# A gated recurrence and a projection block: activation steps of one turn spread over the turns before it

## The chip, the cores and the metric

The kernel runs on one core of a Trainium2 chip. Its time is the device time of one execution in microseconds (us). The kernel before took 618.1 us, the median of three runs (617.54 to 618.85); the profiled run took 618.29 us, with a span of 616.6 us from its first instruction to its last.

## The reference

Two blocks follow one another, all in float32.

```
q, k, v, f_logit: (4, 8, 768, 48)        f = sigmoid(f_logit)
state = 0                                 per batch and head, 48 x 48
for t in 0 .. 767:
    state = f[t][:, None] * state + k[t][:, None] * v[t][None, :]
    y[t]  = q[t] @ state
x   = y, heads side by side: (3072, 384)
h   = x @ w_in                            (384 x 2048)
g   = h * erf(softplus(h))
out = g @ w_out                           (2048 x 384)
```

The weights w_in and w_out arrive as float64, and the kernel receives their words as pairs of 32-bit integers; it turns them into float32 itself, and the text calls that rounding.

## The kernel before, in words

**Tiling.** The 3072 rows are cut into 24 chunks of 128 tokens (index g) and 12 blocks of two chunks (index blk). A chunk goes through four stages. `stage_d` (L381) multiplies the logarithms of the gates with a triangle to sum them, takes two exponentials on ScalarE (`dp`, `kd`, L390 and L393) and scales q and k on VectorE (L402, L406); from chunk 3 on it also copies rows of `dp` to `Tall` by small transfers (L398). `stage_t` (L410) transposes both on TensorE (L418) and copies the result out of PSUM on ScalarE (`qA`, L425; `kT`, L427 or, from chunk 9, VectorE at L429); ahead of that it finishes the state of the chunk before (`next_state`, L445 and L446). `stage_s` (L450) computes scores and state contributions (L467, L475). Chunks 3 to 9 have the scores copied on ScalarE (L495) and masked on GpSimd (L498), later ones on VectorE (L503). `stage_y` (L511) computes y (L532), which ScalarE copies into `xT` (L536). The tiles of `stage_t` and `stage_y` come from a PSUM pool of two buffers, `ps_at`, so that y(g) uses the buffer that L425 of stage_t(g+1) has emptied.

**The second block.** `hidden(blk, gi)` (L585) computes a group of four 128-wide slices of h for 256 rows, 12 matmul steps (L594), and ScalarE copies it to SBUF (L601). A group is named (blk, gi), with gi from 0 to 3. Its PSUM pool `ps_moe` has two buffers. The function h * erf(softplus(h)) is computed from one exponential, three tanh and three products by `activate` (L546): exp (L157), two tanh terms (L160), two products on VectorE (`times`, L165), three empty steps, a last tanh (L566) and the product that ends in h (L568). The tile `e` has two buffers, so the exp of a group waits for the last product of the group two before it. `project_first` (L673, blocks 0 and 1) multiplies h with w_out plainly (L684); `project` (L701, later blocks) uses a scheme of seven products instead of eight (L735), for which `sum_w` and `sum_h` form sums on VectorE (L622). The sums of w_out go to the tile `wT`, over the h of block 0, which lies there too.

**What sets the order.** The order on each engine is written out by hand in one long loop (from L937). Its turn `it` runs from 0 to 11. In a turn a generator gives out matmul steps, called slots (counter `s`). Turn 0 computes hidden(0) and hidden(1) in 96 slots, turn 1 hidden(2) in 48, turn 2 hidden(3) in 48 and then project_first(0) in 32, turn 3 project_first(1) in 32 and then hidden(4) in 48; later turns hold project(it - 2) and hidden(it + 1). After each slot the loop may emit other work:
- a weight-rounding step (`weights_step`, L851), when the counter `due` reaches 1. A piece of a weight matrix (there are 8 of each) takes an absolute value on ScalarE (L311) and six operations on VectorE (L313 to L336). The w_in pieces have to be done ahead of the hidden groups that use them, the w_out pieces ahead of project_first.
- a load of a w_out piece (`load_more`, L868, L292), if the place where its raw words go is free.
- one stage of the recurrence, from the list `todo` at the slots in `at`.
- the logarithms of a later block's gates (`clamp`, L357, on VectorE and `logs`, L363, on ScalarE). Logarithm and tanh need different tables in ScalarE, which are loaded where they change (`ACT_TABLE_LOAD`, at L347 and L160).
- a step of the activations (`act_step`, L574). A step moves every running group on by one operation. A new group starts when the last one has made five steps, so in the long run five steps carry one group.
- from turn 2 on, a step of the sums (`sum_step`, L655).

Where a consumer is reached and its group isn't finished, the steps that it lacks are emitted at that place:

```
while not gr["done"]:
    act_step()
```

This stands in `project_first` (L682) and in `sum_h` (L642).

Of the kernel before, what the change touches and what calls it, by code (L numbers as in the profile page):

```python
# [74 lines left out]
def kernel(  # L75
# [741 lines left out]
    with tc.manual_schedule():  # L817

        for t in svs:
            nc.vector.memset(t[:].rearrange("p r c a d -> p (r c a d)"), 0.0)  # L820
        use_exp_ln()
        load_f(0)
        load(0, "kv", nc.scalar)
        load(0, "q")
        load_f(1)
        load(1, "qk")
        load_f(2)
        load_piece(0)
        load(1, "v")
        load(2)  # L830
        load_piece(1)
        load_piece(2)
        load_f(3)
        nc.gpsimd.memset(tri[:], 1.0)
        nc.gpsimd.affine_select(
            out=tri[:], in_=tri[:], pattern=[[1, P]], compare_op=ALU.is_ge, fill=0.0,
            base=0, channel_multiplier=-1,
        )
        nc.gpsimd.memset(tri[0:C, C:P], 0.0)
        for c in range(2):  # L840
            nc.gpsimd.tensor_copy(out=tri1[half(c), :], in_=tri[half(c), half(c)])
        make_identity(nc, ident)
        for t in dps:
            nc.vector.memset(t[:, :, D:DP], 1.0)
        for t in [qd] + kds:
            nc.vector.memset(t[:, :, D:DP], 0.0)

        to_round = deque(ORDER)
        in_work = []

        def weights_step():  # L851

            if not in_work or len(in_work) == 1 and in_work[0][2] == 5:
                if to_round:
                    i = to_round.popleft()
                    in_work.append([round_piece(i), i, 1])
                    next(in_work[-1][0], None)
            if in_work:
                r = in_work[0]
                r[2] += 1  # L860
                if next(r[0], "end") == "end":
                    rounded.add(r[1])
                    in_work.pop(0)


        to_load = [n_pieces + j for j in (3, 4, 0, 5, 1, 6, 2, 7)]

        def load_more():  # L868
            if to_load and home_free(to_load[0]):
                load_piece(to_load.pop(0))  # L870

        def load_to(g):
            while loaded[0] <= min(g, n_chunks - 1):
                load(loaded[0])
                loaded[0] += 1


        LOOK = 3
        loaded = [2 * LOOK]
        def weights_steps(n):  # L880
            for _ in range(n):
                weights_step()

        busy.append(ps_moe.tile([P, 2, 512], FP32, name="busy", tag="moe")[:, 0, 0:P])
        keep_busy(10)
        prepare(0, 0, 1)
        stage_d(0)
        keep_busy(6)
        prepare(0, 1, 2)
        stage_t(0)  # L890
        load(3, "qk")
        load_piece(3)
        stage_d(1)
        prepare(1, 0, 1)
        load_f(4)
        load_f(5)
        load_sv(0)
        stage_s(0)
        weights_steps(2)
        stage_t(1)  # L900
        load(4, "qk")
        load_piece(4)
        stage_d(2)
        load_sv(1)
        weights_steps(2)
        stage_y(0)
        load_sv(2)
        load(3, "v")
        load(5, "qk")
        load_piece(5)  # L910
        stage_s(1)
        weights_steps(2)
        stage_t(2)
        stage_y(1)
        prepare(1, 1, CPB)
        load_sv(3)
        load(4, "v")
        load_piece(6)
        weights_steps(4)


        def stages(blk):
            todo = [(stage_s, blk * CPB)] if blk == ADJACENT else []
            for g in range(blk * CPB, (blk + 1) * CPB):
                last = g == n_chunks - 1
                if blk >= ADJACENT:
                    todo += [(stage_y, g)] if last else [(stage_d, g + 1), (stage_t, g + 1), (stage_y_s, g)]
                    continue
                todo += [] if last else [(stage_d, g + 1)]
                todo += [(stage_s, g)]  # L930
                todo += [] if last else [(stage_t, g + 1)]
                todo += [(stage_y, g)]
            return todo

        check = check_decays()
        due = 0.0
        for it in range(n_blocks):  # L937
            gen, n = slots(it)
            if it == 0:
                todo = [(stage_s, 2), (stage_y, 2), (stage_d, 3), (stage_t, 3), (stage_s, 3), (stage_y, 3),  # L940
                        (stage_d, 4), (stage_t, 4), (stage_d, 5), (stage_s, 4), (stage_t, 5),
                        (stage_y, 4)] + stages(2)[4:]
                at = [1, 5, 6, 12, 16, 23, 34, 42, 48, 52, 60, 74, 76, 80, 88, 94]
            else:
                todo = stages(it + 2) if it + 2 < n_blocks else []
                at = [n * x // 48 for x in (2, 6, 11, 17, 25, 29, 34, 41)] if it == 1 else [int(3 + (n - 13) / max(1, len(todo)) * i) for i in range(len(todo))]
            if ADJACENT <= it + 2 < n_blocks:

                at = [0, 1, 15, 24, 31, 52, 66] if it + 2 == ADJACENT else [2, 26, 42, 54, 76, 90]
                at = at[: len(todo)]  # L950
            if it + 3 < n_blocks:
                prepare_at = at[todo.index((stage_d, (it + 3) * CPB))] - 14
            at, todo = deque(at), deque(todo)
            for s, _ in enumerate(gen):
                due += (1 if s < 42 else 0.6 if s < 72 else 0.3) if it == 0 else 0.42 if it == 1 else 0.6
                while due >= 1:
                    weights_step()
                    due -= 1
                if s % 6 == 3:
                    load_more()  # L960
                if at and s == at[0]:
                    at.popleft()
                    f, g = todo.popleft()
                    f(g)
                    if f in (stage_y, stage_y_s):
                        if g + NSV < n_chunks:
                            load_sv(g + NSV)
                        load_to(g + LOOK)
                        if g == 2:
                            load(5, "v")  # L970
                            load_piece(7)
                if it == 0 and s == 14:
                    prepare(2, 0, CPB)
                if it == 0 and s == 9:
                    load_f(6)
                    load_f(7)
                if s == n // 2 and it + 4 < n_blocks:
                    for j in range(CPB):
                        load_f((it + 4) * CPB + j)
                if it + 3 < n_blocks and s == prepare_at - 6:  # L980
                    clamp(it + 3, 0, CPB)
                if it + 3 < n_blocks and s == prepare_at:
                    logs(it + 3, 0, CPB)
                if it < 2:
                    step = it == 1 and s % 6 == 3
                elif it == 2:
                    step = s % 5 in (1, 3)
                elif it == 3:
                    step = s % 7 in (1, 4)
                elif it == n_blocks - 1:  # L990
                    step = s % 3 == 1
                else:
                    step = s % 9 in (2, 6)
                if step:
                    act_step()
                if it == 2:
                    if s % 2:
                        sum_step()
                elif it > 2:
                    if s == n - n_h and it < n_blocks - 1:  # L1000
                        to_sum.extend(sum_h(groups[it - 1, gi]) for gi in range(NS))
                    if it == n_blocks - 1 and s % n_o == 40 and s < 2 * n_o:
                        blk = n_blocks - 2 + s // n_o
                        to_sum.extend(sum_h(groups[blk, gi]) for gi in range(NS))
                    if it == 3:
                        if s % 2:
                            sum_step()
                    elif s < n_o or s % 3 == 0 or it == n_blocks - 1:
                        sum_step()
                if it == n_blocks - 2 and s in (5, 40):  # L1010
                    next(check)
            assert not todo
        assert len(rounded) == 2 * n_pieces
# [213 lines left out]
```

## Time and profile before

| engine | busy us | share of the span |
|---|---|---|
| TensorE, matmul | 588.3 | 95% |
| TensorE, weight load | 514.5 | 83% |
| VectorE | 459.7 | 75% |
| ScalarE | 382.9 | 62% |
| GpSimd | 14.9 | 2% |

TensorE carries 74% of the chain that ended last, VectorE 11% and ScalarE 8%. The largest group of instructions is the hidden matmul (L594), with 264.7 us. The longest wait between compute engines is ScalarE's exp (L157) for VectorE's product (L568), 57.6 us in 31 waits. A hidden slot is two records of L594 in the profile, since each float32 matmul shows twice; the same holds for L684 and L735. An instruction's time is given from its start; the idle time ahead of it stands in brackets in a timeline, with the engine and line that ended it. "issue" means that the profile shows no releaser.

### The profile page before, as it was taken

How to read it: one execution, taken by the hardware profiler on the slowest of the kernel's cores; microseconds unless marked ns; L12 is line 12 of the kernel's file. 1: busy time of each engine (PE TensorE's matmuls, PEld its weight loads, DVE VectorE, ACT ScalarE, POOL GpSimd, SP SyncE). 2: the span in 40 equal slices, each digit the busy share in tenths (PEclk: the TensorE clock that was granted, in tenths of full speed). 3: DMA queues.
4: the chain of work that ended last, by engine and by line, in shares of the span. 5: the costliest groups of instructions: out<-in, count | busy, mean ns of one | idle time of the engine just before them, and what ended most of it. 6: DMA issues, size and time to landing. Idle time of an engine off the chain costs nothing.

```text
span 616.6 us, 13769 instructions
## 1 busy us (share of the span) xinstructions
PE 588.3 (95%) x5729; PEld 514.5 (83%) x5729; DVE 459.7 (75%) x785; ACT 382.9 (62%) x483; POOL 14.9 (2%) x33
## 2 busy tenths in 40 slices
PE   8778799999999999999999999999999999999996
PEld 7556688887655689989989988988988989989996
DVE  4898998697489597896896875896886795656651
ACT  5735365987875678875866585875775666366000
POOL 1000011010000000000000000000000000000000
PEclk9987899999999999999999999999999999999999
DMA  9998753441241222133133132042130000000000
GB/s 201 248 228 208 199 175 63 71 88 17 53 77 28 41 63 52 25 81 54 33 71 53 32 73 53 14 91 53 15 65 15 3 27 0 28 1 0 27 27 30
DMA packets 155604, 41.36 MB, mean 67 GB/s; under 512 B 147344, under 2 KB 150416, under 8 KB 155536
## 3 DMA queue, kind: packets, MB, share of 16 engines
q1 hardware_dynamic: 153312, 39.82, 29.6%
q8 instruction: 47, 0.77, 0.5%
q10 hardware_dynamic: 2224, 0.59, 0.4%
q14 instruction: 21, 0.17, 0.1%
HBM read 35.59 MB, written 4.72 MB: 65 GB/s over the span
## 4 chain that ended last, share of the span: by engine, by line
PE 74%; DVE 11%; ACT 8%; DMA 3%; issue 2%; SPq 1%; POOL 0%; DVEq 0%; ACTq 0%; POOLq 0%
PE hps L594 31%; PE ops L735 25%; PE ops L684 7%; PE y L532 3%; PE ps_t L418 3%; PE ps_d L387 2%; ACT x L160 2%; PE sc L467 1%; PE sc L475 1%; DVE sv L445 1%; DVE sv L446 1%; DVE w_in_sb L322 1%; DVE Hg L568 1%; DVE w_in_sb L336 1%; PE busy L379 1%
## 5 line engine op out<-in xcount | busy, mean ns | idle before, releaser
L594 PE MATMUL hps<-xT,w_in_sb 128*128 128x256 f32 x1152 | 264.7, 386 | 5.0 <-DVE w_in_sb L336 2.9
L594 PEld LDWEIGHTS hps<-xT,w_in_sb 128*128 128x128 f32 x1152 | 218.5, 193 | 39.2 <-ACT xT L536 2.8
L165 DVE SCALAR_TENSOR_TENSOR e<-x,e 128x1024 f32<-128x1024 f32 x96 | 117.1, 1220 | 13.2 <-ACT x L160 12.6
L160 ACT ACTIVATE x<-Hg,serf_bias 128x1024 f32<-128x1024 f32 x88 | 97.5, 1140 | 0.2
L157 ACT ACTIVATE e<-Hg 128x1024 f32<-128x1024 f32 x44 | 46.5, 1058 | 61.7 <-DVE Hg L568 57.6
L735 PE MATMUL ops<-wT,Hg 128*128 128x192 f32 x320 | 78.4, 328 | 0.0
L568 DVE TENSOR_TENSOR Hg<-Hg,e 128x1024 f32<-128x1024 f32 x44 | 53.7, 1222 | 22.6 <-ACT e L566 22.5
L735 PE MATMUL ops<-wT,scratch 128*128 128x192 f32 x288 | 67.8, 326 | 0.9 <-DVE scratch L743 0.9
L735 PE MATMUL ops<-w_out_sb,Hg 128*128 128x192 f32 x320 | 65.1, 326 | 0.0
L601 ACT COPY Hg<-hps 128x1024 f32<-128x1024 f32 x44 | 44.4, 1010 | 32.7 <-PE hps L594 32.4
L735 PEld LDWEIGHTS ops<-wT,Hg 128*128 128x128 f32 x320 | 55.7, 190 | 1.9
L735 PEld LDWEIGHTS ops<-w_out_sb,Hg 128*128 128x128 f32 x320 | 54.6, 190 | 2.0
L566 ACT ACTIVATE e<-e 128x1024 f32<-128x1024 f32 x48 | 50.3, 1048 | 1.9 <-DVE e L165 1.8
L735 PEld LDWEIGHTS ops<-wT,scratch 128*128 128x128 f32 x288 | 50.2, 190 | 1.1 <-issue 1.1
L503 DVE TENSOR_TENSOR qA<-sc,tri 64x256 f32<-64x256 f32 x68 | 28.7, 422 | 27.3 <-PE sc L475 26.3
L743 DVE TENSOR_TENSOR scratch<-scratch,ops 128x384 f32<-128x384 f32 (+1 forms) x41 | 20.3, 494 | 29.5 <-ACT scratch L751 23.0
L532 PEld LDWEIGHTS y<-qA,sv 128*32 128x32 f32 x1536 | 24.9, 113 | 19.6 <-issue 12.4
L532 PE MATMUL y<-qA,sv 128*32 128x64 f32 x1536 | 29.9, 226 | 10.9 <-issue 5.1
L425 ACT COPY qA<-ps_t 64x512 f32<-64x512 f32 x48 | 27.7, 577 | 19.4 <-PE ps_t L418 19.0
L402 DVE TENSOR_TENSOR qd<-qn,dp 128x384 f32<-128x384 f32 x24 | 13.4, 556 | 33.6 <-ACT dp L390 33.5
L735 PE MATMUL ops<-w_out_sb,scratch 128*128 128x192 f32 x144 | 34.7, 326 | 0.0
L445 DVE TENSOR_TENSOR sv<-sc,sv 48x192 f32<-48x192 f32 x80 | 28.3, 354 | 8.3 <-ACT qA L495 6.9
(111 smaller groups left out, 648.1 us busy)
## 6 DMA issues: line engine op xcount, KB each, us to landing
lt<-in_f_logit_dram SPq DMA_DIRECT2D x24, 192.0 KB, 3.7
qn<-in_q_dram SPq DMA_DIRECT2D x24, 192.0 KB, 3.4
kn<-in_k_dram SPq DMA_DIRECT2D x23, 192.0 KB, 3.7
vt<-in_v_dram SPq DMA_DIRECT2D x23, 192.0 KB, 3.7
out_dram<-scratch SPq DMA_DIRECT2D x11, 384.0 KB, 2.6
sv<-in_v_dram SPq DMA_DIRECT2D x84, 48.0 KB, 2.8
w_out_sb<-in_moe_w_in_dram SPq DMA_DIRECT2D x4, 768.0 KB, 6.1
Hg<-in_moe_w_in_dram SPq DMA_DIRECT2D x4, 768.0 KB, 6.6
```

The lines of the kernel that those rows point to most:

```text
L157: nc.scalar.activation(out=dst[:], in_=h, func=AF.Exp)
L160: nc.scalar.activation(out=dst[:], in_=h, func=AF.Tanh, bias=serf_bias[:, i : i + 1], scale=SERF_KAB[i][0])
L165: nc.vector.scalar_tensor_tensor(out=e[:], in0=x[:], scalar=SERF_KAB[i][2], in1=e[:], op0=ALU.add, op1=ALU.mult)
L445: nc.vector.tensor_tensor(out=new, in0=add, in1=old, op=ALU.add)
L503: nc.vector.tensor_tensor(out=qA[half(1 - r), r, :, half(c)], in0=sc[half(c), r], in1=tri1[half(c)].unsqueeze(1).broadcast_to((C, HP, C)), ...
L532: nc.tensor.matmul(y[M * i : M * (i + 1), kt, half(c)], lhsT=sv[:, r, c, a, o : o + M], rhs=qA[:, r, a, half(c)], start=(n == 0), stop=Tru ...
L566: nc.scalar.activation(out=e[:], in_=e[:], func=AF.Tanh, scale=SERF_C)
L568: nc.vector.tensor_tensor(out=h, in0=h, in1=e[:], op=ALU.mult)
L594: nc.tensor.matmul(hps[:, j, :], lhsT=w_in_sb[:, kt, ft * P : (ft + 1) * P], rhs=xTs[blk][:, kt, :], start=(kt == 0), stop=(kt == n_k - 1),)
L601: nc.scalar.copy(out=gr["h"], in_=hps[:])
L684: nc.tensor.matmul(ops[:, tt, 0:d_model], lhsT=gr["h"][:, j, tt * P : (tt + 1) * P], rhs=w_out_sb[:, ft, :], start=(ft == 0), stop=(ft == ...
L735: nc.tensor.matmul(place[n], lhsT=x[:, j, :], rhs=y, start=(gi == 0 and j == 0 and n in first), stop=(gi == n_g - 1 and j == 1), skip_grou ...
```

## The change

Three settings of the loop change. In turns 0 and 1 activation steps are emitted where there were none or fewer: in turn 0 from slot 72 on at every eighth slot, in turn 1 at every fifth instead of every sixth. Turn 2 takes the rule of turn 3: two of seven slots instead of two of five. The aim is to even ScalarE's work out over the turns. Loads of w_out are tried in every odd slot instead of every sixth. Rounding goes at half a step per slot in turns 1 and 2, instead of 0.42 and 0.6.

```diff
-                due += (1 if s < 42 else 0.6 if s < 72 else 0.3) if it == 0 else 0.42 if it == 1 else 0.6
+                due += (1 if s < 42 else 0.6 if s < 72 else 0.3) if it == 0 else 0.5
                 while due >= 1:
                     weights_step()
                     due -= 1
-                if s % 6 == 3:
+                if s % 2:
                     load_more()
...
-                if it < 2:
-                    step = it == 1 and s % 6 == 3
-                elif it == 2:
-                    step = s % 5 in (1, 3)
-                elif it == 3:
+                if it == 0:
+                    step = s >= 72 and s % 8 == 5
+                elif it == 1:
+                    step = s % 5 == 3
+                elif it < 4:
                     step = s % 7 in (1, 4)
```

## Prediction

> **What bounds the kernel now.** I read the slices first. TensorE's first six slices (to about 92 us) hold sevens and eights while VectorE stands at 8 to 9; from then on TensorE is at 9 nearly everywhere.
>
> ```profile
> PE   8778799999999999999999999999999999999996
> ...
> DVE  4898998697489597896896875896886795656651
> ACT  5735365987875678875866585875775666366000
> ```
>
> So time can be won or lost only where TensorE waits. Next came busy times over turns 0 to 3, cut where the first matmul of a turn starts (columns: window; its length; busy us of PE, PEld, DVE, ACT, POOL; clock; DMA share; GB/s).
>
> ```profile
> 39.30:105.50 66.20, 58.94 (x590) 48.19 (x588) 62.00 (x99) 35.03 (x57) 5.56 (x8) 0.91 0.67 169
> 105.50:134.90 29.40, 28.98 (x374) 24.19 (x373) 20.95 (x37) 27.01 (x39) 3.15 (x4) 1.00 0.42 73
> 134.90:189.40 54.50, 50.59 (x438) 36.38 (x437) 39.68 (x58) 42.43 (x52) 2.99 (x4) 1.00 0.28 50
> 189.40:239.60 50.20, 50.20 (x486) 37.35 (x485) 39.10 (x64) 36.37 (x42) 0.50 (x2) 1.00 0.27 56
> ```
>
> Turn 0 belongs to VectorE: 62.00 of 66.20 us, nearly all weight rounding, which the change doesn't reduce. Turn 1 costs TensorE 0.42 us, turn 3 nothing. Turn 2 is where it stands idle, with ScalarE as the cause. In the timeline, y(8) (L532) starts when the copy L425 of stage_t(9) ends, because its PSUM buffer is the one that L425 empties; L425 stands behind an exponential, which waited 2.44 us for a product:
>
> ```profile
> 149.45 1.06 ACT L157 ACTIVATE e<-wT 128x1024 f32<-128x1024 f32 x1 [2.44 <-DVE wT L568]
> ...
> 150.51 1.17 ACT L425 COPY qA<-ps_t 64x512 f32<-64x512 f32 x2
> ...
> 151.78 1.37 PE L532 MATMUL y<-qA,sv 128*32 128x64 f32 x64 [1.37 <-issue]
> ```
>
> y(9) at 176.36 waits 1.51 us in the same way. A slot is two matmul records: 0.4317 us in hidden (96 records in 20.72 us), 0.648 us in project_first (28 in 9.03). One d, s, t and y take 0.65, 1.0, 0.87, 1.03. Turn 2 without a wait: 48 x 0.4317 + 32 x 0.648 + 2 x 3.55 = 48.6 us. It takes 54.5, so 5.9 us are lost: 3.8 before project_first starts at 164.67, 2.1 after.
>
> **What the skill says.** "TensorE: Matmul & The Clock Gate", Architectural detail: VectorE and ScalarE queues are strictly first in, first out; the 2.44 us above, passed on to L425, agrees. "ScalarE: Activation LUTs", What ACT_TABLE_LOAD costs: about 1.28 us to load, 1.38 more to drain; here a load takes 1.28 and the next instruction follows 0.02 later, so I use 1.28. The same page, Table sets: exponential and logarithm share one set, exponential and tanh another; so a logs call (L347) between two tanh costs two loads, as the trace shows (203.47, 207.43).
>
> **The change part by part.**
>
> *w_out's loads.* Slots 9 to 51 become 7 to 33. No abs (L311) or rounding step of w_out in the trace waited for a transfer, so nothing is won. Against that, about 4.6 MB are queued from 59.6 us ahead of stage_d(4)'s Tall rows; at 240 GB/s (the window's rate) they are gone at about 79, and the rows land near 81 instead of 77. Needed at 83.54 (L445): hidden, cost 0, at worst 3.
>
> *Rounding.* 0.42 to 0.5 steps per slot ends it at slot 37 of turn 1, not 44. Seven steps of 0.5 to 1.0 us come earlier on VectorE; their cost is in T2 below.
>
> *Steps moved.* I counted them slot by slot with the loop's conditions. Turn 0 gets 3 (0 before), turn 1 gets 9 (8), turn 2 gets 23 (32). Turn 0: exp at slot 77 and two tanh terms at 85 and 93, 1.06 + 1.28 + 1.16 + 1.16 = 4.7 us on ScalarE from 95 to 105, into gaps of 1.87, 1.55 and 2.28 us; L425 of stage_t(6) slips 0.9 but y(5) at 104.00 still finds it done. Cost 0. ScalarE's table loads stay equal in number.
>
> Turn 1, laid out by hand from these durations: L425 of stage_t(7) ends near 115.9, so y(6) no longer waits (-0.42). At the end, exp(1,0) at slot 38 waits for the product of (0,0), which VectorE finishes near 134.1; xT of y(7) is behind it and lands at 135.6 instead of 133.06. Turn 2's first matmul reads it. T2 = 135.7 against 134.92: +0.8 net. Bounds: -0.4 to +1.5.
>
> Turn 2, first part: 14 steps instead of 19 in 48 slots leave ScalarE 11 operations of 1.05 us instead of 15. L425 of stage_t(9) ends near 148.3 with y(8) due at 150.7; the copy of h(3,1) is done at 154.6, needed at 154.8. So 3.5 of the 3.8 us come back; y(9) is free too.
>
> *A wait that the change adds.* project_first's loop runs act_step until its group is done. Before, (0,3) was done at slot 66, needed at 72. With 23 steps it still lacks two. At slot 72 they are emitted immediately ahead of the matmul: tanh, then on VectorE sum_w(2)'s first step (slot 71, overwriting a part of wT that slot 69's matmul reads), times (L165) of (1,2), then the product (L568). From slot 69's end, 1.3 us before slot 72: 0.15 + 0.55 + 1.14 + 1.22 = 3.06, so TensorE stands 1.85 us with the release. If sum_w must wait for slot 71 it is 3.15. Nothing of before shows this wait; I take 1.85, since slot-wise addresses decide it. TensorE's queue behind it holds the rest of project_first. Turn 2's second part: 2.1 lost before, 1.85 now.
>
> T3 = 135.7 + 25.9 + 0.3 + 22.5 + 1.85 = 186.25 against 189.44: 3.2 us ahead.
>
> *A second one, larger.* Before, (1,3)'s tanh is at slot 11 of turn 3, ahead of logs(6) at slot 17. Now it is at slot 22, behind it, and its product is forced at slot 24, where project_first(1) needs it. ScalarE before, after stage_t(11):
>
> ```profile
> 202.28 1.17 ACT L425 COPY qA<-ps_t 64x512 f32<-64x512 f32 x2 [4.69 <-PE ps_t L418]
> 203.47 1.28 ACT L347 ACT_TABLE_LOAD   x1
> 204.76 0.84 ACT L367 ACTIVATE lt<-lt 128x768 f32<-128x768 f32 x1
> 205.64 0.84 ACT L368 ACTIVATE lt<-lt 128x768 f32<-128x768 f32 x1
> ...
> 207.43 1.28 ACT L160 ACT_TABLE_LOAD   x1
> 208.73 1.15 ACT L160 ACTIVATE x<-Hg,serf_bias 128x1024 f32<-128x1024 f32 x1
> ```
>
> Afterwards: L425 1.19, term 1.12, load 1.29, logs 1.65, load 1.29, term 1.06, tanh 1.04 = 8.64 from L425's start, then the product and two hand-overs, 1.4: 10.0. L425 starts 0.7 after stage_t, so slot 24 can start 10.7 us after it; TensorE gets there after 0.87 + 8 x 0.648 = 6.06. Wait: 4.65 us (bounds 3.8 to 5.5). It is tied to stage_t(11), so ScalarE can't work ahead of it.
>
> *A third, passed on.* term and tanh of groups (2,1) and (2,0) now follow the output copy L694 and d(12) (slots 32 and 33), which wait for TensorE, instead of running before. exp(2,2) comes 1.35 us later against TensorE, and the ping-pong exp, tanh, product keeps that lag until L425 of stage_t(12). Before, that copy was just in time:
>
> ```profile
> 230.38 1.15 ACT L425 COPY qA<-ps_t 64x512 f32<-64x512 f32 x2
> ...
> 231.71 0.81 PE L532 MATMUL y<-qA,sv 128*32 128x64 f32 x42
> ```
>
> With 0.1 slack: +1.25 (bounds 0 to 2). From slot 36 of turn 3 the orders are equal, and nothing more differs.
>
> Sum: -3.2 + 4.65 + 1.25 = +2.7. 618.1 + 2.7 = 620.8 us.
>
> **Rivals.**
> - *Forced steps find everything ready* (ends faster): each costs one product and hand-over, 1.3. Recovered 5.9 - 0.3 - 0.8 = 4.8, minus 2.6, minus 1.25: 617.1. For it: ScalarE idles 4.69 us before 202.28. Against: the chain starts only after stage_t(11).
> - *A wash*: xT of y(7) in time (-0.8) and no third wait (-1.25): 618.7, down to 618.1 with a shorter second wait.
> - *More is lost*: sum_w waits for slot 71 (+1.3) and turn 2's copies of h lag on (+1): 623.1.
> - *Loads collide*: Tall rows late, VectorE's queue and turn 0 shift by 3: 623.8. Against: 2 us of slack, and most of the shift would be absorbed where VectorE waits 3.01 us at 108.5.
>
> **How the numbers follow.** Forecast 0.64, more is lost 0.12, loads collide 0.04, wash 0.11, all ready 0.09. The likeliest gives 620.8. Its own terms reach from 619.3 to 622.5; with the wash below and the larger loss above the range is 618.5 to 623.4. Faster by over 0.2% (under 616.9): 0.06. Within 0.2% (to 619.3): 0.13. Slower: 0.81.
>
> **What would show it.** Right: idle TensorE of 4 to 5 us in front of project_first(1)'s last group, released by L568; one of 2 to 3 in front of project_first(0)'s last group; no wait ahead of y(8) and y(9); ScalarE's tanh of (1,3) behind the two table loads; L532 of y(11) waiting for L425. Wrong: the product of (1,3) ends before stage_t(11); or y(8) still waits; or turn 0 ends at another time than 105.5.

## The result and the profile after

The changed kernel takes 621.8 us (median of 4 runs, 621.25 to 622.39) against 618.12 us before. The ratio is 1.0059, with a 95% interval of 1.0042 to 1.0077: 3.7 us slower, where the prediction had 2.7 us in a range of 618.5 to 623.4.

The slices of the span show little, because the changes are small against a slice of 15.5 us. TensorE's row now has a 7 in the fourteenth slice, and the row of the granted clock, which the prediction did not look at, has an 8 at the same place.

```profile
PE   8778799999999799999999999999999999999996
...
PEclk9987899999999899999999999999999999999999
```

A clock of 0.50 in the text below means that TensorE was granted half of its full speed.

The windows of the prediction, on the new trace (window; its length; busy us of PE, PEld, DVE, ACT, POOL; clock; DMA share; GB/s):

```profile
39.30:105.50 66.20, 58.99 (x590) 48.34 (x588) 62.02 (x99) 39.39 (x61) 5.58 (x8) 0.90 0.64 167
105.50:134.90 29.40, 29.17 (x374) 23.91 (x372) 23.03 (x36) 24.03 (x37) 3.08 (x4) 1.00 0.42 73
134.90:189.40 54.50, 53.22 (x508) 38.45 (x508) 38.35 (x62) 39.36 (x52) 3.80 (x4) 1.00 0.30 57
189.40:239.60 50.20, 44.44 (x396) 32.39 (x395) 34.66 (x55) 33.34 (x38) 0.50 (x2) 0.97 0.18 35
```

ScalarE took on 4.4 us in turn 0 (35.03 to 39.39) at no cost to TensorE: d(7) starts at 107.12 us, before at 107.13. In the third window TensorE has 508 instructions instead of 438. Most of its idle time has moved into the fourth window: 5.8 us there, where it had none, and 1.3 us left in the third.

TensorE's timeline has all the waits that matter in a few lines. The number in brackets is the idle time ahead of a piece, with what ended it.

```profile
135.41 2.00 PE L594 MATMUL hps<-xT,w_in_sb 128*128 128x256 f32 x8 [0.29 <-ACT xT L536]
...
150.82 1.10 PE L532 MATMUL y<-qA,sv 128*32 128x64 f32 x64
...
161.99 4.03 PE L684 MATMUL ops<-w_out_sb,wT 128*128 128x384 f32 x12
...
171.99 1.10 PE L532 MATMUL y<-qA,sv 128*32 128x64 f32 x64
173.02 6.72 PE L684 MATMUL ops<-w_out_sb,wT 128*128 128x384 f32 x20
180.72 5.43 PE L684 MATMUL ops<-w_out_sb,wT 128*128 128x384 f32 x16 [0.99 <-DVE wT L568]
185.99 0.81 PE L684 MATMUL ops<-w_out_sb,Hg 128*128 128x384 f32 x2
...
199.01 5.33 PE L684 MATMUL ops<-w_out_sb,Hg 128*128 128x384 f32 x16
208.92 1.65 PE L684 MATMUL ops<-w_out_sb,Hg 128*128 128x384 f32 x2 [4.58 <-DVE Hg L568]
210.50 1.94 PE L532 MATMUL y<-qA,sv 128*32 128x64 f32 x64
...
235.92 1.10 PE L532 MATMUL y<-qA,sv 128*32 128x64 f32 x64 [1.17 <-ACT qA L425]
```

y(8) and y(9), at 150.82 and 171.99, no longer wait; project_first starts at 161.99 instead of 164.67 and turn 3 at 185.99 instead of 189.44. That is the gain. The losses follow: 1.2 us at 180.72 (due at 173.02 + 10 x 0.648 = 179.50), 4.7 us at 208.92 (due at 199.01 + 8 x 0.648 = 204.19), and 1.2 us at 235.92. There is a fourth: the two matmul records at 208.92 need 1.65 us where two records of the same shape need 0.91 elsewhere (the x2 piece at 187.71), and y(10) needs 1.94 us against 1.10 for y(9). The window from 208.92 us has the reason in its clock column:

```profile
204.20:208.90 4.70, 0.14 (x1) 0.00 (x0) 1.26 (x2) 3.38 (x4) 0.00 (x0) 1.00 0.00 0
208.92:212.36 3.44, 3.44 (x66) 2.19 (x66) 1.08 (x1) 0.00 (x0) 0.50 (x2) 0.50 0.00 0
212.40:220.00 7.60, 7.60 (x75) 5.26 (x72) 3.72 (x10) 4.32 (x7) 0.00 (x0) 1.00 0.56 110
```

After 4.7 us without work TensorE ran 3.44 us at a clock of 0.50, so 1.72 us were lost behind the wait.

ScalarE's part of the second wait, on the changed kernel, answers to the lines at 202.28 us of before:

```profile
198.83 1.17 ACT L425 COPY qA<-ps_t 64x512 f32<-64x512 f32 x2 [1.84 <-PE ps_t L418]
200.03 1.15 ACT L160 ACTIVATE x<-Hg,serf_bias 128x1024 f32<-128x1024 f32 x1
201.19 1.28 ACT L347 ACT_TABLE_LOAD   x1
...
204.22 1.28 ACT L160 ACT_TABLE_LOAD   x1
205.51 1.15 ACT L160 ACTIVATE x<-Hg,serf_bias 128x1024 f32<-128x1024 f32 x1
206.57 1.04 ACT L566 ACTIVATE e<-e 128x1024 f32<-128x1024 f32 x1
```

The tanh of (1,3), the last line, stands behind two table loads; the product follows at 207.64 on VectorE and TensorE at 208.92.

### The profile page after: what moved, and what is told of

Its sections match the earlier page's. It is cut to its first block, busy times and chain, and to the rows that moved or that the text cites. A ratio compares the mean times of both kernels' runs of the same rounds, so it can differ in the third digit from the quotient of the medians.

```text
span 620.6 us, 13769 instructions
## 1 busy us (share of the span) xinstructions
PE 589.7 (95%) x5729; PEld 515.4 (83%) x5729; DVE 459.9 (74%) x785; ACT 382.4 (62%) x483; POOL 15.7 (3%) x33
## 4 chain that ended last, share of the span: by engine, by line
PE 75%; DVE 10%; ACT 8%; DMA 2%; SPq 2%; issue 1%; POOL 0%; DVEq 0%; ACTq 0%; POOLq 0%
PE hps L594 33%; PE ops L735 25%; PE ops L684 5%; PE y L532 3%; PE ps_t L418 3%; ACT x L160 2%; PE ps_d L387 2%; PE sc L467 1%; PE sc L475 1%; DVE Hg L568 1%; ACT e L566 1%; ACT e L157 1%; DMA kn<-in_k_dram 1%; SPq L398 1%; DVE w_in_sb L336 1%
## 5 line engine op out<-in xcount | busy, mean ns | idle before, releaser
L532 PEld LDWEIGHTS y<-qA,sv 128*32 128x32 f32 x1536 | 25.2, 116 | 17.8 <-issue 9.1
L532 PE MATMUL y<-qA,sv 128*32 128x64 f32 x1536 | 30.2, 230 | 8.8 <-ACT qA L425 2.4
L425 ACT COPY qA<-ps_t 64x512 f32<-64x512 f32 x48 | 27.7, 576 | 16.0 <-PE ps_t L418 15.6
```

What stands on the lines that cost most here:

```text
L532: nc.tensor.matmul(y[M * i : M * (i + 1), kt, half(c)], lhsT=sv[:, r, c, a, o : o + M], rhs=qA[:, r, a, half(c)], start=(n == 0), stop=Tru ...
```

## The experiments

The theory after the result: at stage_t(11) the change is still 3.45 us ahead, with the first wait of 1.2 us already taken off; it then loses more than that to two further waits (one of them, like the first, in front of a matmul whose group is finished by forced steps, the other ahead of y(11)) and to the half clock behind the longest. The rivals: the new loads, the rounding or the early steps cost the time; or the waits have other causes than those named.

Each time below is a median, with the ratio to the kernel before on the same chip and its interval. Since the profiled executions differ by up to 2.7 us ahead of d(6) and by up to 2 us behind y(11), also between kernels that are alike there, the table also gives a narrower measure, from the one trace of each kernel: from the start of d(6) (L387, at 93.45 us before) to the start of y(11) (L532, at 231.71). It holds the last slots of turn 0, all of turns 1 and 2, and turn 3 up to the point from which the orders are equal.

| kernel | median us | ratio, interval | d(6) to y(11), us | against before |
|---|---|---|---|---|
| before | 618.1 | | 138.26 | |
| changed | 621.8 | 1.0059 (1.0042 to 1.0077) | 142.48 | +4.22 |
| turn 2's old rule | 614.88 | 0.9943 (0.9930 to 0.9956) | 134.95 | -3.31 |
| logs later | 617.95 | 1.0002 (0.9993 to 1.0010) | 137.66 | -0.60 |
| wait filled | 620.83 | 1.0038 (1.0024 to 1.0051) | 140.93 | +2.67 |
| loads and rounding alone | 619.21 | 1.0019 (1.0008 to 1.0030) | 138.97 | +0.71 |
| steps of turns 0 and 1 alone | 616.53 | 0.9974 (0.9964 to 0.9983) | 136.45 | -1.81 |
| steps ahead of the copy | 621.40 | 1.0059 (1.0040 to 1.0078) | 141.12 | +2.86 |
| turn 2's rule alone | 628.31 | 1.0170 (1.0142 to 1.0198) | 148.33 | +10.07 |
| dense second part | 612.89 | 0.9919 (0.9899 to 0.9939) | 133.58 | -4.68 |
| ... with old loads | 612.99 | 0.9916 (0.9903 to 0.9929) | 133.58 | -4.68 |
| ... with old rounding | 612.69 | 0.9906 (0.9893 to 0.9918) | 133.71 | -4.55 |
| ... with exp after y | 613.26 | 0.9912 (0.9899 to 0.9925) | 133.03 | -5.23 |
| sum step later | 620.99 | 1.0052 (1.0039 to 1.0065) | 141.21 | +2.95 |

**Turn 2's old rule in the changed kernel.**

```diff
-                elif it < 4:
+                elif it == 2:
+                    step = s % 5 in (1, 3)
+                elif it == 3:
                     step = s % 7 in (1, 4)
```

> The changed kernel with turn 2's old step rule (two of five slots); the steps of turns 0 and 1, the loads and the rounding stay changed. No step is forced then: the product of (0,3) comes at slot 56 of turn 2, that of (1,3) at slot 1 of turn 3. Theory (the loss is made by the steps that project_first forces, and by what follows them): no waits ahead of the last groups of both project_first, no half clock, no wait of y(11), but turn 2's first part loses its 3 to 4 us again: 617 to 618.5 us. Rival (the steps of turns 0 and 1, the loads or the rounding cost the time): stays at 620.5 to 622.

It took 614.88 us, faster than both kernels and than the theory had it. The forced waits are gone, and with them the half clock and y(11)'s wait, as expected. But turn 2 did not lose its old 3 to 4 us: y(8) starts at 151.09 and y(9) at 173.64 without a wait, and only 0.8 us are idle ahead of project_first. ScalarE has no less to do in turn 2 than before. From the first matmul of turn 2 to the first of turn 3 (this run, then before; columns as above):

```profile
135.67:186.38 50.71, 49.86 (x436) 36.15 (x437) 39.36 (x59) 43.69 (x54) 3.79 (x4) 1.00 0.30 53
134.92:189.44 54.52, 50.61 (x439) 36.36 (x437) 39.70 (x58) 42.43 (x52) 2.99 (x4) 1.00 0.28 50
```

Its timeline shows what is different:

```profile
147.84 1.04 ACT L566 ACTIVATE e<-e 128x1024 f32<-128x1024 f32 x1
148.91 1.18 ACT L425 COPY qA<-ps_t 64x512 f32<-64x512 f32 x2
150.29 1.06 ACT L157 ACTIVATE e<-Hg 128x1024 f32<-128x1024 f32 x1 [0.20 <-DVE Hg L568]
```

With the earlier steps the cycle of five has shifted: L425 now comes ahead of the exp that waits for a product, and before it came behind. So the loss of before did not come from the amount of work alone. That it came from the place of a waiting instruction in the queue is read from these two traces; no run moves that exp by itself.

**The logs of turn 3 later.**

```diff
+                if it == 3:
+                    prepare_at += 8
```

> The changed kernel with turn 3's logs (and their clamp) eight slots later, at slot 25 instead of 17, so that the tanh of (1,3) at slot 22 is no longer behind two table loads and the logarithms. Theory (the logs in front of the tanh make the second wait): 4.2 of the 4.75 us of the wait go, and the 1.7 us at half clock behind it; d(12) and what follows may come up to 1 us later: 616 to 617.5 us. Rival (the wait comes from the product being forced at slot 24 at all): within 1 us of 621.8.

The wait at slot 24 fell from 4.7 to about 0.4 us and the half clock behind it went: y(10) starts at 205.36 instead of 210.50. So the two table loads and the logarithms in front of the tanh made the wait. The median, 617.95 us, came 0.5 us above what was expected, because the third wait grew: y(11) waits 2.33 us instead of 1.17. The same loads and logarithms are now ahead of the chain that ends in that copy.

```profile
231.11 1.10 PE L532 MATMUL y<-qA,sv 128*32 128x64 f32 x64 [2.33 <-ACT qA L425]
```

**The wait filled with matmuls of no use.** The kernel computes them in addition; its output is not touched.

```diff
+                    if blk == 1 and gi == n_g - 1 and tt == 0 and j == 0:
+                        fill = ps_at.tile([P, 512], FP32, name="fill", tag="at")
+                        for _ in range(20):
+                            nc.tensor.matmul(fill[:, 0:P], lhsT=tri[:], rhs=tri[:], start=True, stop=True)
                     nc.tensor.matmul(
                         ops[:, tt, 0:d_model],
```

> The changed kernel with 20 matmuls of no use (128 columns each, some 4.4 us together, into a PSUM tile that nobody reads) ahead of the first matmul of project_first(1)'s last group, where TensorE waits 4.75 us. Theory (the 1.7 us lost behind the wait are a clock that falls to half because TensorE stands idle): the wait is filled, the clock stays at 1.00, 1.5 to 1.9 us come back: 620.0 to 620.3 us. Rival (the slow matmuls behind the wait have another cause, such as their operands): 621.8 us and a stretch at half speed as before.

```profile
204.11 4.63 PE L687 MATMUL fill<-tri 128*128 128x128 f32 x40
208.86 0.91 PE L688 MATMUL ops<-w_out_sb,Hg 128*128 128x384 f32 x2
209.71 1.10 PE L532 MATMUL y<-qA,sv 128*32 128x64 f32 x64
```

The matmul that waited still starts at 208.86, but it and y(10) run at full speed, with a clock of 1.00 from 208.86 to 212.00. The stretch is 1.55 us shorter than the changed kernel's (140.93 against 142.48), about what the half clock had cost. The median fell by 1.0 us, but the two intervals overlap, so it is the trace that shows it. The slow matmuls come from the idle time, not from their operands.

**Loads and rounding alone**, on the kernel before.

```diff
-it == 0 else 0.42 if it == 1 else 0.6
+it == 0 else 0.5
-                if s % 6 == 3:
+                if s % 2:
                     load_more()
```

> The kernel before with the new rules of w_out's loads and of the rounding alone; activation steps as before. Theory (both are hidden, since no rounding step waited for a load and the rounding ends ahead of its use): 618.1 us, within 0.8. Rival (the earlier loads delay the rows of Tall and with them VectorE and turn 0): 620 to 622 us, turn 0 ending up to 3 us later.

It took 619.21 us, 0.7 us more in the stretch, with an interval that lies above 1: outside what the theory allowed. Turn 0 ends as before (d(7) at 107.14), so the rival's cause is wrong too. y(6) waits 1.22 us instead of 0.42. ScalarE's timeline shows an absolute value of the rounding (L311) ahead of L425, where the faster rate has put it:

```profile
115.64 0.91 ACT L311 ACTIVATE w_out_sb<-scratch 128x768 f32<-128x768 f32 x1
116.45 1.15 ACT L425 COPY qA<-ps_t 64x512 f32<-64x512 f32 x2
```

In the changed kernel the same L311 stands there, but the exp and the term of (0,0) have left for turn 0, L425 starts at 114.76, and y(6) at 116.39 does not wait.

**The steps of turns 0 and 1 alone**, on the kernel before: the two branches for `it == 0` and `it == 1` of the change, and nothing else.

> The kernel before with the new activation steps of turns 0 and 1 alone: turn 2's rule, the loads and the rounding are the old ones. Theory (these steps are what gains; loads and rounding are hidden once ScalarE's steps have left turn 1's crowded stretch): as fast as the changed kernel with turn 2's old rule, 614.9 us within 0.8. Rival (loads and rounding cost the 1.2 us that they cost alone): 613 to 614 us.

They win 1.81 us of the stretch, less than the 3.31 of the version that has the new loads and rounding too. The theory had expected no difference and the rival a cost of loads and rounding: they cost 0.7 us alone, and are worth 1.5 us here. In this trace an exp waits 3.86 us for a product that stands behind the last rounding steps on VectorE, and y(8) waits 0.85 us.

```profile
142.80 1.06 ACT L157 ACTIVATE e<-wT 128x1024 f32<-128x1024 f32 x1 [3.86 <-DVE wT L568]
```

**Turn 3's steps ahead of the output copy.**

```diff
+                elif it == 3 and 25 <= s <= 32:
+                    step = s in (25, 27, 29, 30)
                 elif it < 4:
                     step = s % 7 in (1, 4)
```

> The changed kernel with turn 3's steps at slots 25, 27, 29 and 30 in place of 25, 29 and 32, so that a term and a tanh come ahead of the output copy L694 of slot 31 instead of behind it. Theory (the wait of y(11) comes from these two behind the copy): y(11) doesn't wait, 1.2 us less, 620.6 us. Rival (the lag is that of the 4.75 us wait itself): y(11) waits as before, 621.8 us.

The edit puts a term and a tanh ahead of the copy L694; it also has four steps in these slots where the changed kernel has three.

```profile
215.48 1.04 ACT L566 ACTIVATE e<-e 128x1024 f32<-128x1024 f32 x1
217.69 0.80 ACT L694 COPY scratch<-ops 128x768 f32<-128x768 f32 x1 [1.16 <-PE ops L684]
```

y(11) no longer waits, though the second wait stays (4.6 us), and the stretch from y(10) to y(11) is 24.05 us instead of 25.42. So the steps' place around that copy made the third wait, not the lag of the second. The median of 621.40 us with its interval can't show 1.2 us; the trace does.

**Turn 2's rule alone**, on the kernel before.

> The kernel before with turn 2's new step rule alone; turns 0 and 1 have the old, fewer steps. Theory (forced steps make the loss, and the steps of turns 0 and 1 hold it down): six rounds of steps are forced at slot 72 with an exp, two terms and a tanh one after another behind sum_w, a wait of some 6 us and a half clock behind it (1.7), then the same second wait, half clock and y(11) wait as in the changed kernel (7.7); the gain of turn 2 is 5.5: 626 to 629 us. Rival (turn 2's rule costs no more than in the changed kernel, since ScalarE has time): 620 to 623 us.

628.31 us. TensorE waits at slot 72 until 183.61 us (due at 178.15: 5.5 us), then runs 3.5 us at a clock of 0.52, and the second and third waits follow as in the changed kernel.

```profile
183.61 7.12 PE L684 MATMUL ops<-w_out_sb,wT 128*128 128x384 f32 x16 [5.22 <-DVE wT L568]
```

The steps of turns 0 and 1 and turn 2's rule belong together: the fewer steps come before, the more are forced.

**A dense second part.** Turn 2 keeps the sparse rule while ScalarE has copies of h to make, and has a step in every second slot after that.

```diff
+                elif it == 2:
+                    step = s % 7 in (1, 4) if s < n_h else s % 2 == 1
```

> The changed kernel with turn 2's new rule for the 48 slots of hidden and every second slot for the 32 of project_first, where ScalarE has no h to copy. No step is forced in front of project_first and the tanh of (1,3) comes at slot 4 of turn 3, ahead of the logs. Theory: the hidden part keeps its gain, both forced waits go; turn 3 starts near 184.8 us and nothing is lost behind it: 612.5 to 614 us, below the one with turn 2's old rule (614.9). Rival (denser steps crowd the copies L425 and make y wait): 615 us or more.

612.89 us, the fastest with its variants: 0.8% below the kernel before (interval 0.6 to 1.0%). Turn 3 starts at 184.95, and no wait is left ahead of either last group or y(11).

**The fastest version with old loads, old rounding, or the exp after y.** The first two undo one line of the change; the third replaces turn 1's rule:

```diff
-                    step = s % 5 == 3
+                    step = s % 5 == 3 and s < 38 or s in (42, 46)
```

> The fastest version so far (turn 2's new rule for hidden, every second slot for project_first; 612.9 us) with the old rule of w_out's loads, every sixth slot. Theory (no rounding step waits for a load): 612.9 us within 0.8. Rival (early loads help, since the steps alone took 1.6 us longer without the new loads and rounding): 614 to 615 us.

> The same fastest version with the old rounding rate (0.42 in turn 1, 0.6 after). Theory (rounding steps left at the end of turn 1 stand on VectorE ahead of the product of (0,1), for which exp(0,2) waits; here that exp comes later, at slot 11, so the half microsecond is hidden): 612.9 us within 0.8. Rival (it costs here what it seems to cost with turn 2's old rule): 614 to 615 us, with y(8) waiting again.

> The same fastest version with the last two steps of turn 1 at slots 42 and 46 instead of 38 and 43, so that exp(1,0), which waits for the product of (0,0), comes behind the copy of y(7) into xT instead of ahead of it. Theory (that wait delays turn 2's first matmul by 0.6 us): turn 2 starts 0.5 us earlier against y(7), 612.4 us. Rival (something else holds the start back, or the two later steps cost as much elsewhere): 612.9 us or more.

Old loads give the same stretch to the last digit (133.58), old rounding one that differs by 0.13. But the execution with old rounding took 14.17 us from d(6) to d(7), where these kernels are still alike and all the others took 13.67 or 13.68. Counted from d(7) to y(11) it took 119.54 us against 119.90 of the fastest version: the old rounding is 0.36 us shorter there, all of it ahead of turn 2, where VectorE finishes the product of (0,0) that much earlier. So the new loads are worth nothing in this version, and the new rounding costs some 0.4 us, as one trace has it; the medians can't show so little.

With the exp after y, xT of y(7) is written as soon as y(7) is there, turn 2 starts without a wait, and the stretch is 0.55 us shorter.

```profile
131.93 0.48 ACT L536 COPY xT<-y 128x384 f32<-128x384 f32 x1 [0.38 <-PE y L532]
133.45 1.06 ACT L157 ACTIVATE e<-Hg 128x1024 f32<-128x1024 f32 x1 [1.03 <-DVE wT L568]
```

Its median, 613.26, doesn't show it; the spread of the executions (611.87 to 613.79) is wider.

**The sum step of slot 71 later**, in the changed kernel.

```diff
-                    if s % 2:
+                    if s % 2 and s != 71:
                         sum_step()
```

> The changed kernel without the sum step of slot 71 in turn 2 (it follows at slot 73), so that times (1,2) and the product of (0,3) no longer stand behind sum_w(2), which waits for TensorE. Theory (this place in VectorE's queue makes the first forced wait): the 1.2 us wait at slot 72 of turn 2 is gone, all else as in the changed kernel: 620.6 us. Rival (the forced tanh is late in itself): the wait stays, 621.8 us.

The wait at slot 72 of turn 2 is gone and the stretch 1.27 us shorter; the other waits stay. The first wait came from the product's place behind sum_w(2) on VectorE, not from a late tanh. The median, 620.99, is near the 620.6 expected, but its interval also holds the changed kernel's ratio.

The second wait is as long here as in the changed kernel, yet the matmul behind it still runs at full speed, and the half clock starts 0.8 us later:

```profile
206.96:207.80 0.84, 0.84 (x2) 0.29 (x2) 0.84 (x1) 0.00 (x0) 0.00 (x0) 0.98 0.00 0
207.80:211.30 3.50, 3.50 (x113) 3.26 (x113) 0.24 (x1) 1.47 (x3) 0.50 (x2) 0.52 0.10 20
```

## Why the prediction was right

The direction, the waits and their causes were right. That the measured time still fell inside the range is in part luck: a term of 1.7 us was missing, and the spread that had been allowed for other terms covered it.

- *The start of turn 2* (T2): 135.41 us for 135.7. The copy of y(7) into xT came behind the exp, as laid out; in the fastest version, moving the exp gave 0.55 us back.
- *Turn 2's first part*: project_first starts at 161.99, for 135.7 + 25.9 + 0.3 = 161.9. The stretch took 26.6 us where 26.2 had been laid out, and the earlier T2 made up for it. y(8) and y(9) are free.
- *The first forced wait*: right in kind, 1.2 us for 1.85 (the list of signs had said 2 to 3, which does not fit its own sum). The mis-sized term is the release of sum_w: it was taken from slot 69's end, and VectorE starts it at 177.84, which is 0.3 us after the end of slot 68 (173.02 + 7 x 0.648 = 177.56). sum_w writes the first 384 words of a group, and of the slots that read these, slot 68 is the last.
- *Turn 3*: 185.99 for 186.25.
- *The second forced wait*: 4.7 us for 4.65, from the chain that was named; taking the logs out of it took the wait away.
- *The third, at y(11)*: 1.2 us for 1.25, from the order that was named.
- *Loads at no cost*: right. *Rounding*, whose cost the prediction put into T2: 0.36 us of T2 are its, by the comparison of old and new rounding above. On the kernel before, the two together cost 0.7 us, from a place that the prediction did not look at.
- *What was missing*: the half clock. The sum had -3.2 + 4.65 + 1.25 = +2.7 us; the trace has -3.45 at stage_t(11), then +4.7, +1.7 at half clock and +1.2, which is 4.2 us at y(11). The Trainium skill, "TensorE: Matmul & The Clock Gate", What's actually happening, says that an idle window of about 3.4 us brings the clock to one half, until a busy window of that length. A forecast wait of 4.65 us should have been read together with it. This trace agrees: 4.7 us idle, then 3.44 us at 0.50. Waits of 1.2 us had no such effect.

The kernel before shows the price too, in turn 0, in the window whose clock of 0.91 stands among the prediction's lines. stage_t(4) waits there for VectorE, and what follows runs at half clock:

```profile
72.26 1.03 PE L418 MATMUL ps_t<-ident,qd 128*128 128x128 f32 x4 [3.16 <-DVE qd L402]
...
72.26:75.66 3.40, 3.40 (x13) 3.04 (x14) 3.30 (x6) 2.30 (x4) 0.00 (x0) 0.51 0.31 56
```

By its bracket this wait is a little shorter than the window that the page names, and two waits of 2.6 us at the same place in other runs were followed by clocks of 0.70 and 1.00: in these traces the length of a wait alone does not decide.

The rivals fell one by one. Forced steps do not find everything ready: the second wait was 4.7 us. It was no wash: xT of y(7) was late and the third wait came. No more was lost in the way that "more is lost" had it: sum_w waited for slot 68, not 71, and project_first started without waiting for a copy of h. The loads did not collide: turn 0 ends within 0.01 us of before. The range of the forecast's own terms, 619.3 to 622.5, is given without its working; the bounds of the terms of T2 and of the second and third waits, added up, reach from 617.5 to 623.1.

One reading of the kernel before was too simple. The prediction saw the exp that waits ahead of L425, but took the gain from fewer operations of ScalarE in turn 2. The version with turn 2's old rule has as much of that work and loses little, so the order of L425 and the waiting exp counts as well.

What stays open: why loads and rounding are worth 1.5 us with turn 2's old rule was read from one trace and not taken apart. That the loads are worth nothing was shown in the fastest version only.

## What to carry to other kernels

When steps are taken out of a hand-written order, look for the places that finish unfinished work by force: what they emit stands directly ahead of its consumer, and whatever stands in front of it on its engine becomes the consumer's wait. Ask for each moved operation which table load, which copy that waits for TensorE, and which write that waits for a reader it now stands behind. Where a long wait of TensorE is forecast, look in the traces at hand for one of that length and read the clock behind it: here a wait of 4.7 us cost some 1.6 us beyond its length, since the matmuls behind it ran at half speed for 3.4 us.

## What the runs showed of the hardware

- A TensorE that stood idle 4.7 us (changed kernel) or 5.5 us (turn 2's rule alone) then ran at a clock of 0.50 and 0.52 for 3.4 to 3.5 us; in turns 1 to 3, single waits up to 2.3 us (y(11) with the logs later) left it at 1.00. Matmuls whose result nobody reads kept it at 1.00.
- The wait of stage_t(4) in turn 0 differs between the profiled executions of the 14 kernels. Behind the twelve waits of 3.1 to 5.6 us the mean clock of the next 3.4 us was 0.50 to 0.60; behind the two of 2.6 us it was 0.70 and 1.00. So waits of equal length came out differently.
- Short waits close together can do the same: in turn 0 of the kernel before, y(3) waits 1.69 us and, four matmul records later, 0.41 us, and from 55.2 to 62.0 us the clock is 0.51. In the run with turn 2's rule alone the same two waits left it at 1.00.
- The same operations at another place in a queue go with no wait or with one of 1 to 2 us, at no less busy time: with turn 2's old rule and the earlier steps, ScalarE is busy 43.69 us in turn 2, against 42.43 before, and turn 2 is 3.8 us shorter.
